# The first slice's first product taken by quarters of K between the heads of the first attention, on 512 columns

## The chip, the cores and the metric

The kernel runs on one core of a Trainium2 chip. Its time is the device time of one execution in microseconds (us), the median of several runs. TensorE multiplies (its weight loads run beside its matmuls and have rows of their own, PEld), VectorE (DVE), ScalarE (ACT) and GpSimd (POOL) do the elementwise work, and all DMAs are issued from SyncE (SP).

## What is computed

Three stages follow each other on 1152 tokens (2 batches of 576) and 512 features:

```python
scores = q @ k.T / 8                       # 2 batches, 8 heads, 576 positions, 64 wide
mask: heads 0-3: 0 <= rel < 32
      heads 4-7: 0 <= rel < 128 and rel % 4 == 0
x = softmax(scores) @ v                    # -> [1152, 512]
p = domain_probs / (domain_probs.sum(-1) + 1e-9)
x = sum over 4 experts e of p[:, e] * (relu(x @ w1[e]) @ w2[e])     # 512 -> 1024 -> 512
h = x @ w_in                               # 512 -> 2048; float64 weights
out = (h - tanh(h)) @ w_out
```

## The kernel before

**Precision and tiles.** Matmuls are in float32r. Each operand is split into a high part (a rounded copy) and a low part (the rest), and three matmuls, high x high, high x low and low x high, make one exact one. The tokens stand in two sets: 512 (g = 0) and 640 (g = 1). The two layers are cut into slices of 512 hidden features: 8 slices of the first layer pair, 4 of the second. In a slice the first product gives the hidden features, 4 tiles f of 128, and the second product (steps `y`) multiplies them with w2 into a sum per token block. The slices 0 and 1 (`EARLY`) are done for g = 0 alone first, with their first product taken whole (`whole`, L1177); later slices use a seven-product scheme (`product`, L1216) on differences of quarter blocks, whose operands t1 to t4 are prepared by `prep_upper` and `prep_lower` (L734, L742).

**The first attention.** The 8 heads of g = 0 stand in four pairs, two plain ones and two dilated ones. For a pair `scores` (L920) makes 32 small matmuls into two PSUM banks; `softmax` (L937) runs per head over DVE, ACT and POOL; `transposes` (L966) first issues 4 or 6 dummy matmuls on zeros (`keep_warm`, L903) and then 4 transposes, whose result ACT copies out; `values` (L995) multiplies with v, and ACT copies the result to `xf`. A pair gives one quarter of K (kk = 0 to 3) of x for the products. `first_attention` (L1422) writes the order out: scores of pairs 0 and 1, the transposes of head 0, the scores of pair 2, the transposes of heads 1 and 2, the scores of pair 3, the values of pair 0, and so on. Only after that does `prep_whole` (L755) split x into four operands of two halves of 256 tokens each: ACT copies the high part, DVE subtracts for the low part.

**The first product.** `whole(n, f, half)` takes one f and one half of the tokens: 4 quarters of K x 3 matmuls of 256 columns, 8 such groups per slice, and after the second half a relu that is split again (ACT and DVE). It needs all four quarters of x.

**Weights.** `w_load` (L1051) loads 512 KB at a time into a ring of four raw tiles; `w1_split` (L1079) copies the high part on ACT and subtracts on POOL.

**The order of the work.** All operations are recorded first and then ordered by a planner (`Order`, L353). TensorE's order is the program's; on the other engines `lay` (L414) picks, at each step, by an operation's due time (`late`), which `deadlines` (L378) counts back from TensorE's running sum. Costs are a model in `Engine.cost` (L319). The second attention (g = 1) and other work off TensorE's main line are put between the steps with `when(due, ...)` (L1398, L1465 to L1487): `due` is a time in the plan's own sum of step durations, counted from the first product's start, and the work goes ahead of the first step that begins at or after it.

```python
        if n < EARLY:
            return 1.44
        return 6 * (0.120, 0.146)[g]
...
    BEAT = 10.5
    for n in range(4):
        pair = Pair(kinds[1, n < 2], n % 2)
        due = 9.0 + BEAT * n
...
        when(due + 12.2, pair.last)
        for i in range(2):
            when(due + 13.8 + 1.6 * i, lambda pair=pair, i=i: pair.values(i))
```

Of the kernel before, what the change touches and what calls it, by code (L numbers as in the profile page):

```python
# [103 lines left out]
class Tile:  # L104


    def __init__(self, ring, shape, dtype, hosts=()):
# [4 lines left out]
        self.hosts = hosts  # L112
# [16 lines left out]
class View:  # L129
# [46 lines left out]

    def region(self):
# [25 lines left out]
class Op:  # L203
    __slots__ = (
        "n", "engine", "us", "emit", "before", "after", "tiles", "port", "late", "ready", "left",
        "start", "end", "landing", "tail", "data",
# [6 lines left out]
class Program:  # L213
# [3 lines left out]
    DMA_US, DMA_RATE, DMA_AHEAD = 2.0, 300.0e3, 0.36  # L217

    def __init__(self):
        self.ops = []  # L220
        self.open = None

    def op(self, engine, us, emit, outs=(), ins=(), port=False, data=0.0):
# [9 lines left out]
        o.before, o.after, o.tiles = set(), [], []  # L233
        o.tail = self.TAIL[engine]
# [61 lines left out]
class Engine:  # L296
# [22 lines left out]
    def cost(self, method, kw, outs, ins):  # L319
# [25 lines left out]
        if method == "tensor_tensor":  # L345
            return 0.185 + n * 0.00217, True
# [3 lines left out]
NAMES = ("tensor", "vector", "scalar", "gpsimd", "sync")  # L350


class Order:  # L353
# [6 lines left out]
    def __init__(self, program, rounds=3):  # L360
# [12 lines left out]
        self.follow = None  # L373
        for _ in range(rounds):
            self.deadlines()
            self.lay()

# [36 lines left out]
    def lay(self):  # L414

        ops = self.ops
        free = dict.fromkeys(NAMES, 0.0)
        port = path = 0.0
        lag = 0.0
        for ring in self.rings:  # L420
            ring.next = 0
            ring.free = [(0.0, i, None) for i in range(len(ring.slots))]
        for o in ops:
# [6 lines left out]
            o.start = o.end = None  # L430
        follow = {}
        waiting = {name: [o for o in ops if o.engine == name and not o.left] for name in NAMES}
        pe = [o for o in ops if o.engine == "tensor"]
        pe_next, done = 0, 0
        while done < len(ops):
            best = None
            for name in NAMES:
                if name == "tensor":
                    if pe_next == len(pe) or pe[pe_next].left:
                        continue  # L440
                    able = [pe[pe_next]]
# [3 lines left out]
                for o in able:  # L445
                    at = max(o.ready, free[name])
                    claims = {}
                    for t in o.tiles:
                        if t.slot_n is None:
# [3 lines left out]
                            if (  # L453
                                ring.next + k >= len(ring.tiles) or ring.tiles[ring.next + k] is not t
                                or k >= len(ring.free)
                            ):
# [8 lines left out]
                if not found:  # L465
                    continue
                first = min(f[0] for f in found)
                pick = min((f for f in found if f[0] <= first + 0.03), key=lambda f: f[1:3])
                if name != "tensor":
                    end = pick[0] + pick[3].us  # L470
                    for f in found:
                        if (
                            f[0] < end and f[1] < pick[1] - 0.5
                            and end > f[1] + lag - self.AHEAD
                            and pick[1] + lag > f[0] + f[3].us + pick[3].us * 0
                        ):
                            if best is None or True:
# [1128 lines left out]
```

## Time and profile before

| | |
|---|---|
| median of 3 runs | 632.15 us (631.94 to 632.74) |
| profiled execution | 632.89 us, span 631.1 us |
| TensorE busy | 620.2 us (98% of the span), 4093 matmuls |
| DVE, ACT, POOL busy | 406.6, 303.4, 332.7 us (64%, 48%, 53%) |
| DMA | 68.05 MB, mean 108 GB/s |
| mean granted TensorE clock | 0.996 |

The profiled execution's span runs from its first to its last instruction; the time of a run holds 1.8 us more around it. A busy share counts an engine's instructions, dummies among them, and matmul ends are modelled, so the pace of TensorE is read from starts of matmuls or of weight loads. Nearly all operations are emitted from one helper, line 312, so groups are told apart by tile names and shapes: `att` holds softmax tiles, `x` operands of x (and q and k before), `w` split weights, `h` hidden features (and v before), `acc` the plain x and later the sums, `raw` loaded weights.

### The profile page before, as it was taken

The page shows a single profiled execution, that of the slowest core. Times are in us where ns is not written, and L with a number is a line of the kernel's source. Part 1 is how long each engine was busy: PE and PEld are TensorE (multiplying, and loading weights), DVE is VectorE, ACT ScalarE, POOL GpSimd, SP SyncE. Part 2 cuts the span into 40 slices and gives each one's busy share as a digit, 9 for nine tenths or more (in the row PEclk, how much of TensorE's full clock was granted, in tenths as well). Part 3 has the DMA queues.
Part 4 walks back from the last instruction along what each step waited for, and adds up shares of the span by engine and source line. Part 5 has one row for each costly group of instructions (what it writes and reads, how often), then busy time and mean ns, then how long its engine had stood idle before and what let it go on. Part 6 is the DMA issues. An engine that isn't in the chain of part 4 may idle for free.

```text
span 631.1 us, 10738 instructions
## 1 busy us (share of the span) xinstructions
PE 620.2 (98%) x4093; PEld 545.6 (86%) x4093; DVE 406.6 (64%) x727; ACT 303.4 (48%) x720; POOL 332.7 (53%) x292
## 2 busy tenths in 40 slices
PE   7999999999999999999999999999999999999997
PEld 3598888989889889889889889898798988998985
DVE  5696647888987798725425458245998973653652
ACT  4758666456325325415315346353785661651540
POOL 5458876567524425524424448873476782570320
PEclk8999999999999999999999999999999999999999
DMA  8982216336465365112112112231507511200012
GB/s 322 346 268 58 78 38 198 102 119 215 134 186 175 113 201 166 62 51 66 35 34 68 33 34 68 83 114 73 166 11 215 160 50 51 68 1 1 18 51 83
DMA packets 36691, 68.05 MB, mean 108 GB/s; under 512 B 4128, under 2 KB 10400, under 8 KB 36640
## 3 DMA queue, kind: packets, MB, share of 16 engines
q1 hardware_dynamic: 36640, 67.37, 33.0%
q8 instruction: 32, 0.52, 0.3%
q14 instruction: 19, 0.16, 0.1%
HBM read 56.61 MB, written 10.75 MB: 107 GB/s over the span
## 4 chain that ended last, share of the span: by engine, by line
PE 85%; DVE 8%; POOL 2%; DMA 2%; ACT 1%; issue 1%; DVEq 0%; SPq 0%; POOLq 0%; ACTq 0%
PE bank L312 85%; DVE att L312 4%; DVE bank L312 1%; DVE x L312 1%; POOL h L312 1%; DMA att<-in_moe_w_out_dram 1%; DVE h L312 1%; DMA in<-att 1%; ACT att L312 1%; POOL att L312 0%; ACT h L312 0%; DVE w L312 0%; DVE st L312 0%; POOL w L312 0%; POOL sum L312 0%
## 5 line engine op out<-in xcount | busy, mean ns | idle before, releaser
L312 PE MATMUL bank<-w,h 128*128 128x512 f32 (+1 forms) x1392 | 322.1, 384 | 0.9 <-ACT h L312 0.7
L312 PE MATMUL bank<-x,w 128*128 128x256 f32 (+1 forms) x2040 | 288.3, 296 | 1.1 <-DVE bank L312 0.5
L312 PEld LDWEIGHTS bank<-x,w 128*128 128x128 f32 x2040 | 280.6, 189 | 9.7 <-DVE bank L312 0.9
L312 PEld LDWEIGHTS bank<-w,h 128*128 128x128 f32 (+1 forms) x1392 | 241.0, 185 | 51.6 <-POOL h L312 1.3
L312 POOL TENSOR_TENSOR w<-raw,w 128x512 fp32r<-128x512 f32 x102 | 139.0, 1379 | 138.1 <-ACT w L312 137.0
L312 ACT ACTIVATE h<-bank 128x320 fp32r<-128x320 f32 (+4 forms) x164 | 68.3, 427 | 88.3 <-PE bank L312 73.3
L312 DVE SCALAR_TENSOR_TENSOR acc<-bank,pn,acc 128x512 f32<-128x512 f32 x63 | 47.1, 749 | 76.4 <-PE bank L312 76.2
L312 DVE SCALAR_TENSOR_TENSOR att<-att 128x512 int32<-128x512 int32 (+1 forms) x96 | 89.5, 941 | 2.1
L312 ACT ACTIVATE w<-raw 128x512 fp32r<-128x512 f32 x112 | 69.0, 627 | 33.0 <-PE bank L312 30.6
L312 DVE TENSOR_TENSOR bank<-bank,p 128x320 f32<-128x320 f32 (+1 forms) x132 | 61.0, 466 | 32.2 <-PE bank L312 21.6
L312 DVE SCALAR_TENSOR_TENSOR h<-bank,h 128x320 fp32r<-128x320 f32 (+2 forms) x120 | 55.5, 474 | 21.8 <-ACT h L312 20.0
L312 POOL TENSOR_TENSOR w<-sum,w 128x512 fp32r<-128x512 f32 x36 | 47.7, 1324 | 37.1 <-ACT w L312 37.0
L312 ACT ACTIVATE p<-bank 128x320 f32<-128x320 f32 (+1 forms) x88 | 35.9, 412 | 55.4 <-PE bank L312 54.3
L312 ACT ACTIVATE att<-bank 128x256 f32<-128x256 f32 (+3 forms) x78 | 32.9, 433 | 50.1 <-PE bank L312 45.9
L312 POOL TENSOR_TENSOR h<-att,h 128x256 fp32r<-128x256 f32 (+1 forms) x32 | 30.4, 964 | 32.7 <-ACT h L312 32.0
L312 ACT ACTIVATE att<-att 128x512 f32<-128x512 f32 (+2 forms) x40 | 26.1, 652 | 35.4 <-DVE att L312 30.7
L312 DVE TENSOR_TENSOR acc<-bank,acc 128x512 f32<-128x512 f32 (+1 forms) x28 | 18.7, 672 | 36.3 <-PE bank L312 36.1
L312 POOL TENSOR_TENSOR att<-att,st 128x384 f32<-128x384 f32 (+1 forms) x24 | 21.7, 909 | 24.0 <-DVE st L312 21.8
L312 ACT ACTIVATE w<-sum 128x512 fp32r<-128x512 f32 x36 | 22.6, 626 | 16.4 <-PE bank L312 14.5
L312 POOL TENSOR_TENSOR sum<-raw 128x512 f32<-128x512 f32 x12 | 16.6, 1387 | 25.5 <-issue 8.7
L312 DVE TENSOR_SCALAR att<-att 128x512 int32<-128x512 int32 x32 | 19.0, 597 | 4.1 <-DMA in<-att 3.1
L312 DVE TENSOR_TENSOR bank<-bank,att 128x256 f32<-128x256 f32 (+1 forms) x32 | 14.5, 463 | 10.2 <-ACT att L312 9.8
(56 smaller groups left out, 361.6 us busy)
## 6 DMA issues: line engine op xcount, KB each, us to landing
raw<-in_moe_w_dram SPq DMA_DIRECT2D x40, 512.0 KB, 3.9
att<-in_moe_w_in_dram SPq DMA_DIRECT2D x16, 512.0 KB, 4.2
att<-in_moe_w_out_dram SPq DMA_DIRECT2D x16, 512.0 KB, 4.6
in<-att SPq DMA_DIRECT2D x16, 256.0 KB, 4.3
out<-att SPq DMA_DIRECT2D x16, 256.0 KB, 3.8
raw<-in SPq DMA_DIRECT2D x8, 512.0 KB, 3.8
raw<-out SPq DMA_DIRECT2D x8, 512.0 KB, 3.6
h<-in_v_dram SPq DMA_DIRECT2D x7, 512.0 KB, 7.3
```

Source lines behind the costliest of these rows:

```text
L312: getattr(self.engine, method)(**real)
```

## The change

The first product of slices 0 and 1 runs on 512 columns: x is kept as whole 512-column high and low tiles (`x_whole`), and `whole(n, f, kks)` takes any quarters of K. For slice 0 the quarters 0, 1 and 2 are recorded within the first attention (`some`) and marked as filling work; only quarter 3 follows as steps. Their four PSUM banks are claimed when wanted (`loose`) and stay open until quarter 3. For g = 0, `values` copies the high part from PSUM on ACT, subtracts the low part on DVE, and copies the plain x after that. All scores come ahead of the first transposes. `keep_warm` goes; `warm` records single dummy matmuls that the planner issues or leaves out. The high copies of slice 0's w1 go to DVE. Dilated q and k are loaded in halves, and v stands ahead of the first w1 load. The planner has start times per engine, other DMA constants, picks among the next 40 TensorE operations (filling work if it ends by the time the next fixed one can start), and tries 1200 random shifts of the due times of the operations up to the first product's last step, keeping those with the earliest end.

```diff
-    DMA_US, DMA_RATE, DMA_AHEAD = 2.0, 300.0e3, 0.36
+    DMA_US, DMA_RATE, DMA_AHEAD = 2.2, 360.0e3, 0.4
+
+    BEGIN = {"tensor": 0.9, "vector": 0.8, "scalar": 2.0, "gpsimd": 0.7, "sync": 0.75}
...
         for _ in range(rounds):
             self.deadlines()
             self.lay()
+        self.seek(program.seek, 1200)
+        self.lay()
...
+    def of_tensor(self, pe, found):
+
+        fixed = next((o for o in pe if not o.fill), None)
+        first = [f for f in found if f[3] is fixed]
+        idle = [f for f in found if f[3].fill == "idle"]
+        fill = [f for f in found if f[3].fill is True]
+        pick = first[0] if first else None
+        for some in (fill, idle):
+            if some:
+                f = min(some, key=lambda f: (f[0], f[2]))
+                if pick is None or f[0] + f[3].us <= pick[0] + self.OVER:
+                    pick = f
+        return pick
...
+    def x_whole(kk):
+
+        j = kk // 2
+        if ("whole", j) not in xop[0]:
+            t = [x_tile(0).rearrange("p a b q -> p a (b q)") for _ in range(2)]
+            xop[0]["whole", j] = t
...
-    def keep_warm(bank_, n):
-
+    def warm(n):
+
+        P.fill = "idle"
+        if 0 not in whole_:
+            whole_[0] = bank(True)
...
-                if self.h.g == 0 and (self.kk, a) != (3, 1):
-                    keep_warm(pb, 6 if self.kk == 3 else 4)
...
-            for dst, src in h.evict(i, xb, self.kk):
+            if h.g == 0:
+                hi, lo = x_whole(self.kk)
+                for dst, src in h.evict(i, xb, hi):
+                    copy(dst, src)
+                for (dst, src), (back, _) in zip(h.evict(i, xb, lo), h.evict(i, xb, hi)):
+                    sub(dve, dst, src, back.bitcast(F32))
+            for dst, src in h.evict(i, xb, xf[h.g][self.kk]):
                 copy(dst, src)
...
-        split(t[:, 0], t[:, 1], src, engine)
+        split(t[:, 0], t[:, 1], src, engine, None if n else dve)
...
-    def whole(n, f, half):
...
+    def whole(n, f, kks):
+
+        if f not in whole_:
+            whole_[f] = bank(n == 0)
+        b = whole_[f]
         with P.group():
...
+            for kk in kks:
+                w, x = w1t[n, f"a{f // 2 + 1}{kk // 2 + 1}"], x_whole(kk)
...
-        return [("h", n, g, i) for i in range(8 if n < EARLY else len(ORDER))]
+        return [("h", n, g, i) for i in range(NF if n < EARLY else len(ORDER))]
...
-            return 1.44
+            return 0.227 * (12 if n else 3)
...
-            whole(n, i // 2, i % 2)
+            whole(n, i, range(KD) if n else (3,))
...
+        def some(kk):
+            if not kk:
+                w1_all(0)
+                ready["w1"] = 0
+            P.fill = True
+            for f in range(NF):
+                whole(0, f, (kk,))
+            P.fill = False
+
+        warm(WARM)
         pairs[0].scores()
         soft(0, 1)
         pairs[1].scores()
-        soft(2)
+        soft(2, 3)
+        warm(12)
+        pairs[2].scores()
+        warm(12)
+        pairs[3].scores()
+        soft(4, 5)
+        warm(12)
         turn(0)
-        pairs[2].scores()
-        soft(3)
+        warm(12)
         turn(1)
-        soft(4)
+        warm(12)
         turn(2)
-        pairs[3].scores()
         pairs[0].values(0)
-        soft(5)
+        warm(12)
         turn(3)
-        soft(6)
+        soft(6, 7)
+        some(0)
         turn(4)
         pairs[1].values(0)
-        soft(7)
         turn(5)
         turn(6)
-        prep_whole(0, 0, False)
-        prep_whole(0, 1, False)
+        some(1)
         pairs[2].values(0)
-        prep_whole(0, 0, True)
         turn(7)
         pairs[3].values(0)
-        prep_whole(0, 1, True)
-
+        some(2)
...
-    da.load_q()
-    for u in range(2):
-        da.load_k_cut(u)
+    for c in range(2):
+        da.load_q(slice(c, c + 1))
+        da.load_k_cut(c)
+    for i in range(2):
+        pa.load_v(i)
     w_load(0, 0)
     for i in range(2):
-        pa.load_v(i)
+        da.load_v(i)
     w_load(0, 1)
```

## Rows read from the trace of the kernel before

**Rows 1.** The page: the span in 40 slices, busy tenths.

```profile
PE   7999999999999999999999999999999999999997
...
DMA  8982216336465365112112112231507511200012
```

**Rows 2.** Stretches of 5 us: PE, PEld, DVE, ACT, POOL busy (instructions), clock, DMA share, GB/s.

```profile
10.00:15.00 5.00, 4.37 (x44) 2.52 (x44) 3.80 (x12) 2.43 (x10) 3.13 (x5) 0.66 1.03 404
15.00:20.00 5.00, 5.00 (x82) 3.10 (x80) 2.13 (x6) 2.92 (x11) 2.40 (x3) 1.00 1.02 386
20.00:25.00 5.00, 4.63 (x52) 2.57 (x51) 3.56 (x10) 4.21 (x14) 2.15 (x3) 1.00 1.09 328
25.00:30.00 5.00, 4.22 (x66) 2.87 (x66) 4.56 (x8) 4.43 (x9) 3.60 (x4) 1.00 0.97 333
```

**Rows 3.** The chain that ended last, first 45 us: start, us, what.

```profile
10.63 9.57 PE bank L312 x124
...
32.43 12.71 PE bank L312 x132
```

**Rows 4.** Timeline of TensorE, 5 to 46 us: start, us, operation, idle before.

```profile
10.63 0.64 PE L312 MATMUL bank<-ident,att 128*96 128x128 f32 x4 [2.36 <-POOL att L312]
11.20 1.43 PE L312 MATMUL bank<-x,x 64*64 64x96 f32 x32
12.56 1.89 PE L312 MATMUL bank<-zero 128*32 128x512 bf16 x4
...
16.68 0.89 PE L312 MATMUL bank<-x,x 64*64 64x96 f32 x32
...
20.12 1.04 PE L312 MATMUL bank<-zero 128*32 128x512 bf16 x4
...
21.66 1.15 PE L312 MATMUL bank<-w,h 96*64 96x64 f32 x32
...
30.52 0.97 PE L312 MATMUL bank<-x,w 128*128 128x256 f32 x6
...
41.76 1.05 PE L312 MATMUL bank<-x,x 64*64 64x96 f32 x40
...
44.27 2.03 PE L312 MATMUL bank<-w,h 128*128 128x512 f32 x8
```

**Rows 5.** One stretch of 256-column matmuls: its length and its weight loads (PEld).

```profile
62.26:66.53 4.27, 4.27 (x36) 1.00 0.28 95
```

**Rows 6.** Timeline around the last first-attention copy and the last second-attention values.

```profile
30.63 1.08 ACT L312 ACTIVATE acc<-bank 128x512 f32<-128x512 f32 x1 [0.63 <-PE bank L312]
...
105.15 9.60 PEld L312 LDWEIGHTS bank<-w,h 128*128 128x128 f32 x42
...
113.22 0.48 DVE L312 TENSOR_TENSOR x<-acc,x 128x320 fp32r<-128x320 f32 x1
...
114.80 7.32 PEld L312 LDWEIGHTS bank<-x,w 128*128 128x128 f32 x49
```

**Rows 7.** Groups of DVE, 0 to 36 us: busy us, mean ns, idle before.

```profile
L312 DVE TENSOR_TENSOR x<-acc,x 128x256 fp32r<-128x256 f32 x8 | 3.0, 419 | 1.9 <-ACT x L312 1.8
...
L312 DVE CAST p<-p 128x384 bf16<-128x384 f32 x1 | 0.4, 360 | 1.6 <-POOL p L312 1.6
```

**Rows 8.** Instructions on the weight tiles, 30 to 60 us: ns min/median/max.

```profile
L312 POOL TENSOR_TENSOR w<-raw,w x8: 1279/1290/1759, 33.7 to 58.5; 128x512 fp32r<-128x512 f32 x8
L312 DVE TENSOR_TENSOR w<-raw,w x2: 1239/1422/1606, 37.0 to 41.1; 128x512 fp32r<-128x512 f32 x2
```

**Rows 9.** Timeline of SP: the first issues of weight loads.

```profile
7.00 2.70 SPq L605 DMA_DIRECT2D raw<-in_moe_w_dram  x3
```

**Rows 10.** DMA issues from 7.0 to 8.2 us: KB each, median us to landing.

```profile
raw<-in_moe_w_dram SPq DMA_DIRECT2D x2, 512.0 KB, 10.8
```

**Rows 11.** Timeline of POOL, 40 to 60 us: start, us, operation, idle before.

```profile
47.91 1.01 POOL L312 TENSOR_TENSOR att<-att,st 128x480 f32<-128x480 f32 x1 [4.95 <-DVE st L312]
...
54.77 5.02 POOL L312 TENSOR_TENSOR w<-raw,w 128x512 fp32r<-128x512 f32 x4
```

More of the change, by code (lines that the diff above doesn't have):

```diff
@@ L175, in real, with real_strides @@
         return ap
+    def real_strides(self):
+        at = self.at
+        return [
+            1 if n == 1 else int(np.take(at, 1, axis=i).flat[0] - np.take(at, 0, axis=i).flat[0])
+            for i, n in enumerate(at.shape)
+        ]
     def region(self):
@@ L205 @@
         "n", "engine", "us", "emit", "before", "after", "tiles", "port", "late", "ready", "left",
-        "start", "end", "landing", "tail", "data",
+        "start", "end", "landing", "tail", "data", "fill", "gone",
     )
@@ L345, in cost @@
         if method == "tensor_tensor":
-            return 0.185 + n * 0.00217, True
+            spread = any(0 in v.real_strides() for v in ins)
+            return 0.185 + n * (0.00168 if spread else 0.00217), True
         return 0.1 + n * 0.0025, True
 NAMES = ("tensor", "vector", "scalar", "gpsimd", "sync")
+class Stuck(Exception):
+    pass
 class Order:
@@ L420, in lay @@
         for ring in self.rings:
+            ring.left = [t for t in ring.tiles if not t.loose]
             ring.next = 0
@@ L452, in lay @@
                             claims[ring] += 1
[L453 to L456, printed above, removed]
+                            if k >= len(ring.free) or not (t.loose or (
+                                ring.next + k < len(ring.left) and ring.left[ring.next + k] is t
+                            )):
                                 at = None
@@ L501, in lay @@
                     ring = t.ring
[L502 removed]
+                    ring.next += not t.loose
                     ring.free.sort()
@@ L519, in lay, with leave, stuck @@
             done += 1
-        self.follow = follow
-        self.us = max(o.end for o in ops)
-    def stuck(self, waiting, pe, pe_next):
-        said = [f"pe {pe_next}/{len(pe)} left {pe[pe_next].left if pe_next < len(pe) else None}"]
-        if pe_next < len(pe):
-            said.append(str([(t.ring.name, t.slot_n) for t in pe[pe_next].tiles]))
-            said.append(str([ops.n for ops in (self.ops[b] for b in pe[pe_next].before) if ops.start is None]))
+        if limit is None:
+            self.follow = follow
+        self.us = max(o.end for o in ops if o.engine == "tensor")
+    def leave(self, o, at):
+        o.start = o.end = o.landing = at
+        o.gone = True
+        for t in o.tiles:
+            t.left -= 1
+        for n in o.after:
+            a = self.ops[n]
+            a.left -= 1
+            assert a.engine == "tensor"
+    LOOK = 40
+    OVER = 0.1
+    def of_tensor(self, pe, found):
[8 more added lines that the diff above has]
+                if pick is None or f[0] + f[3].us <= pick[0] + self.OVER:
+                    pick = f
+        return pick
+    def stuck(self, waiting, pe):
+        said = [f"pe {len(pe)} left {pe[0].left if pe else None}"]
+        if pe:
+            said.append(str([(t.ring.name, t.slot_n) for t in pe[0].tiles]))
         for name, found in waiting.items():
@@ L619, in copy, with split @@
         act.activation(out=out, in_=in_, func=ACTF.Copy)
-    def split(hi, lo, src, engine):
-        copy(hi, src)
+    def split(hi, lo, src, engine, first=None):
+        if first is dve:
+            dve.tensor_copy(out=hi, in_=src)
+        else:
+            copy(hi, src)
         sub(engine, lo, src, hi.bitcast(F32))
@@ L981, in transposes @@
             to = self.pt.setdefault(a, t[:, 1])
-            copy(to[:BK], pb[:BK])
+            if False:
+                dve.tensor_copy(out=to[:BK], in_=pb[:BK])
+            else:
+                copy(to[:BK], pb[:BK])
         def last(self):
@@ L1517, in tile_local_attention_moe_tanhshrink @@
     db.load_v_short()
-    idle = bank()
-    with P.group():
-        keep_warm(idle, WARM)
     first_exp = const("first_exp", [128, 32], BF16)
```

148 lines of the change are left out of this document (90 added, 58 removed).

## The prediction, made before the change was run

> **What bounds the kernel now.** I read first the slices of the page [rows 1], to see where TensorE is not full: in the first slices only. The digit is 9 from the third slice to the last but one, and DMA is busy in the first three. Whatever shortens the time must therefore either cut TensorE's work after the head, or move it into the head. The cut by 5 us shows what the head is made of [rows 2]: TensorE shows 4.2 to 5.0 us busy of 5, but at 10 to 15 us at a granted clock of 0.66, and DMA is at its limit (share about 1, 330 to 400 GB/s). The chain of waits [rows 3] then says that the head is not one engine's: softmax steps alternate with a piece of 9.57 us on TensorE, and from 32.43 us on TensorE alone carries the end. The timeline of TensorE [rows 4] shows what those pieces hold: transposes (0.64), scores (0.89; 1.43 in the slow stretch), values (1.15), and between them groups of dummy matmuls on zeros, four taking 1.04 and in the slow stretch 1.89. These dummies are the gap: time in which TensorE is counted busy and does nothing. The first slice's first product begins at 30.52 and ends where the second product begins, at 44.27. Of that, some 1.0 is the scores of the second attention at 41.76, so I call its end E = 43.3, the scores left out.
>
> **The change, part by part.**
>
> *512 columns instead of 2 x 256.* 36 matmuls of 256 columns go from 62.26 to 66.53, 0.1186 each [rows 5]; 42 of 512 columns from 105.15 to 114.80, 0.230 each [rows 6]. The first product of an early slice was 96 x 0.1186 = 11.4 and becomes 48 x 0.230 = 11.0. In the second slice, where nothing else of it changes, that is a gain of 0.3 to 0.4; I take 0.3.
>
> *Three quarters of K moved into the head.* The first slice's product falls into four quarters of 12 x 0.230 = 2.76. Quarters 0, 1 and 2 are filling work: 36 matmuls, 8.3 us, put wherever the next attention step isn't ready. Only the last quarter must follow the last attention output. Two things bound the new E.
>
> From the chain's side: the last values end at about 30.6 and ScalarE copies them out in 1.08 (strided, from 30.63) [rows 6]. After the change that first copy is already the high part, and one VectorE step of 128x512 from PSUM makes the low part; no row shows that step, so it lies between two of the 128x256 steps (2 x 0.42 [rows 7]) and the longest 128x512 step, 1.61 [rows 8]. I take 0.9, nearer to the two halves since they compute the same. So without any shortening of the attention x is ready at 30.63 + 1.08 + 0.9 = 32.6 (high end 33.3), and E = 32.6 + 2.76 = 35.4. How much does the attention itself shorten? The fixed dummies between the transposes leave the order, and all scores come ahead. In the 9.57 us piece of the chain lie three dummy groups (the 1.89 one, and two as the one of 1.04), 3.9 us. All of that gone is one bound, nothing the other; I take 1.6, under the half, because VectorE (4.56 of 5 busy at 25 to 30) and ScalarE (4.43) would be late next [rows 2]. E = 33.8 by this side, 31.5 to 36.1 by its ends.
>
> From TensorE's side: quarter 0 can't start before the first w1 block is in and split. Before, the first loads of w1 are issued at 7.00 [rows 9] and take 10.8 to land [rows 10], so 17.8, plus one copy and one GpSimd step (1.29, with 1.76 at most [rows 8]): 19.7. The change puts the first values' loads ahead of it and the others' behind, so about 1 MB less lies before it (128 x 2048 floats of dilated values), which at the 400 GB/s of [rows 2] is 2.6: about 17. At 17 four transposes and two and a half values are left by my count, 4 x 0.57 (the step from 10.63 to 11.20) + 2.5 x 1.15 = 5.2, and 11.0 of product: 17 + 16.2 = 33.2 if TensorE never idles. From 19.7 with one more pair done it is 34.7. Both sides meet at 33 to 35; I take E = 33.8, a gain of 9.5, with 11.8 and 7.2 as ends.
>
> *The split of w1 and of x.* The four high copies of w1 go from ScalarE to VectorE. No row shows such a copy: between 0.36 (a 128x384 cast) and 1.61 (the longest 128x512 step) [rows 7, 8], so 1.4 to 6.4 for four; I take 2, by the cast, which has one input as they have. Against it stand eight x steps of 0.42 that become four of 0.9: about even. VectorE has to place those 2 us between 10 and 30 us, where it is busy 3.80 + 2.13 + 3.56 + 4.56 of 20 [rows 2]: the 6 us idle are the cover, and if that is gone, the chain's side above gets later by them, which the bound of 36.1 holds. ScalarE copies each output twice, as high part and as plain x; the second copy isn't awaited by the product.
>
> *More, smaller loads.* The dilated q and k come in halves: four more issues on SP, some 0.9 each by the three weight loads of 2.70 [rows 9], ahead of values and weights. The queue's engines are full anyway, so they cost nothing while they stay full; otherwise up to 3.6 on quarter 0, again inside the bound.
>
> *What follows sooner.* The second product of slice 0 starts some 9.5 us earlier, but the second attention's steps are placed by plan time from the start of the first product, so they don't move earlier by as much. Its last values stood 9.65 us before the first product on the second token set: from 105.15 to 114.80 lies most of a second product [rows 6]. In the change the first slice's eight plan steps of 1.44 become four of 0.68, so every later step has a plan time some 9 smaller, and the last values come directly ahead of that first product: the cover is gone. There, 24 matmuls of 320 columns at 7.32 / 49 = 0.15 [rows 6] (3.6 us) remain until the first operand that needs these values. I charge 1.0 for it; the bounds are under rival 1.
>
> *The clock.* TensorE is idle for 2.36 us before 10.63, and the next scores take 1.43 against 0.89 [rows 4]; the stretch has 0.66 granted [rows 2], a mean of the two levels, 1.2 and 2.4 GHz. The change drops the fixed dummies ahead of each transpose and puts dummies only where the planner models a gap. One such dip costs about 1.5 (0.54 of scores, 0.85 of dummies, some of transposes), and I leave the one that is there.
>
> **Sum.** -9.5 - 0.3 + 1.0 = -8.8. The profiled execution took 632.89 (span 631.1 and 1.8 around it), so 624.1; the median of the runs is 0.74 lower, so 623.4. About 0.2%, 1.3 us, is what a measurement of this kernel can tell from no change.
>
> **Rivals.**
>
> 1. *The second attention becomes the wait.* For it: from the last values' end at 105.15 to the end of the last step that prepares the second x at 113.70 (113.22 + 0.48) pass 8.55 [rows 6]; if the awaited operand were the last of them, TensorE would wait 8.55 - 3.6 = 4.9. Against it: the steps ran late there because nothing asked for them. The stall is 0 to 4.9; at about 4 the time is some 626.5, and with E at its late end 629.
>
> 2. *GpSimd holds the second slice.* Its four w1 splits run from 54.77 to 59.79, two are needed for the first group, and that group started about when two were done (54.77 + 2 x 1.25 = 57.3) [rows 11]. If that can't move, TensorE gains at the first product and waits it out there: only 0.3 and some tenths remain, 631.5. Against it: GpSimd idled 4.95 us before 47.91, and the splits had no haste.
>
> 3. *The quarters don't fit.* If the first w1 block lands or is split so late that the quarters run after the last x, the change doesn't do what it says: E = 31.0 + 11.0 = 42.0, and the time is 632.15 - 1.3 - 0.3 = 630.5. For it speak the landing time of 10.8 and the full DMA; against it that 1 MB can go behind.
>
> 4. *The clock falls, slower.* Between 10.6 and E lie 8.9 us of attention and 11.0 of product. If the planned gaps differ from the real ones, TensorE idles as before 10.63 and runs the work at 1.2 GHz. Each microsecond of work so run costs one more, some 3.3 of them in idle time; the change turns to a loss from about 13 us of the 20 on. With 15: 12 more, 635. For it speaks that the only dip of the head came right after an idle stretch, though a dummy group preceded it [rows 4]; against it that from 15 us on the clock held at 1.00 [rows 2], and that the quarters make the head denser. The Trainium skill (TensorE: Matmul & The Clock Gate, "The HAM clock gate") says the throttled state is the default and activity releases it, which speaks against taking dummies out; the dip after idling agrees [rows 2, 4]. By that rule, were the real work too thin, the time would be this rival's.
>
> **How the numbers follow.** Forecast (both sides of E at 33 to 35, small stall): 0.60, own range 619.8 to 626.5. Rival 1: 0.19. Rival 2: 0.06. Rival 3: 0.06. Rival 4: 0.09. Faster is the forecast with rivals 1 and 3, 0.85; no change is rival 2, 0.06; slower is rival 4, 0.09. The range goes from E at 31.5 with no stall (632.15 - 11.8 - 0.3, about 619.8) to E at 36.1 with a stall of 4.4 (632.15 - 7.2 - 0.3 + 4.4 = 629.0); rivals 2 to 4 stay out of it.
>
> **What would show it.** Right: 48 matmuls of 512 columns of the first slice's x and w, 36 of them ahead of the last values; no more than 12 of them after; the second product starting at 34 to 35 instead of 44.27; about the same TensorE pace thereafter, so that every later stage lies 9 us earlier. Rival 1 shows as idle TensorE a few groups into the first product on the second token set, released by VectorE or ScalarE; rival 2 as idle before the second slice's first group, released by GpSimd; rival 3 as a solid 11 us of product after the last values; rival 4 as a granted clock well under 1 from 15 to 35 us. The prediction is wrong if the second product starts after 37, or if the 9 us gained there are not found at the end.

## The result and the profile after

The change made the kernel slower: 638.30 us, median of 4 runs (637.73 to 638.71), beside 632.05 (631.61 to 632.74) for the kernel before; the ratio is 1.0097, with a 95% interval of 1.008 to 1.0115. The profiled execution took 638.29, span 636.5, mean granted clock 0.984 (before: 632.89, 631.1 and 0.996). The forecast was 623.4. Two executions of this document, 675.79 (kernel before) and 755.69 (e10_gate_warm_low_first), ran at a granted clock of 0.85 and 0.754 and are left out of every median.

The slices of the page after, to be laid beside [rows 1] (PEclk is the granted clock in tenths):

```profile
PE   8769999999999999999999999999999999999997
...
PEclk9769999999999999999999999999999999999999
```

The loss is in the head again: the second and third slices of TensorE are lower than they were, and everything behind them is full as before. The stretches of 5 us of the kernel after (columns as in [rows 2]) show when there is a dip, a stretch at the lower clock:

```profile
15.00:20.00 5.00, 2.82 (x43) 1.89 (x41) 4.00 (x10) 3.33 (x12) 3.22 (x4) 0.93 1.03 340
20.00:25.00 5.00, 3.56 (x38) 2.97 (x39) 4.07 (x13) 2.42 (x10) 3.35 (x5) 0.50 1.01 365
25.00:30.00 5.00, 5.00 (x23) 4.07 (x22) 4.27 (x7) 4.37 (x11) 3.04 (x3) 0.88 0.72 223
30.00:35.00 5.00, 3.94 (x48) 2.87 (x46) 2.19 (x6) 2.81 (x4) 1.25 (x2) 1.00 0.74 189
35.00:40.00 5.00, 1.96 (x22) 1.46 (x24) 4.93 (x6) 0.90 (x2) 5.00 (x6) 0.64 0.97 377
40.00:45.00 5.00, 3.82 (x24) 2.65 (x21) 2.37 (x5) 2.00 (x2) 1.28 (x2) 0.50 1.04 401
45.00:50.00 5.00, 5.00 (x13) 3.84 (x13) 1.48 (x3) 2.10 (x4) 0.00 (x0) 0.50 0.59 220
```

From 15 to 25 us TensorE had 5.00 and 4.63 busy of 5 at a clock of 1.00 [rows 2]; now it has 2.82, then 3.56 at a granted 0.50, which is the lower level, 1.2 GHz, throughout. From 35 to 40 us it has 1.96, and the 10 us behind that run at 0.50 again. The timeline of TensorE after, to be laid beside [rows 4], names the places:

```profile
21.44 1.08 PE L324 MATMUL bank<-ident,att 128*96 128x128 f32 x4 [3.61 <-POOL att L324]
22.45 1.98 PE L324 MATMUL bank<-w,h 96*64 96x64 f32 x32
24.36 3.17 PE L324 MATMUL bank<-x,w 128*128 128x512 f32 x9
...
27.72 3.00 PE L324 MATMUL bank<-x,w 128*128 128x512 f32 x12
...
32.17 0.96 PE L324 MATMUL bank<-x,w 128*128 128x512 f32 x3
32.97 0.60 PE L324 MATMUL bank<-ident,att 128*96 128x128 f32 x4
33.44 0.50 PE L324 MATMUL bank<-x,w 128*128 128x512 f32 x1
35.44 0.73 PE L324 MATMUL bank<-x,w 128*128 128x512 f32 x2 [1.50 <-DVE x L324]
36.09 0.33 PE L324 MATMUL bank<-att,h 96*64 96x64 f32 x2
39.03 1.97 PE L324 MATMUL bank<-att,h 96*64 96x64 f32 x30 [2.60 <-ACT att L324]
40.92 2.08 PE L324 MATMUL bank<-x,w 128*128 128x512 f32 x4
44.18 6.89 PE L324 MATMUL bank<-x,w 128*128 128x512 f32 x17 [1.18 <-DVE x L324]
50.91 8.52 PE L324 MATMUL bank<-w,h 128*128 128x512 f32 x36
```

The quarters are there: 9 + 12 + 3 + 1 + 2 + 4 + 17 = 48 matmuls of 512 columns. But TensorE stands still for 3.61 us ahead of head 4's transposes, and the values that follow take 1.98 where they took 1.15 in [rows 4]. It stands still for 2.60 within the last values, between the first 2 of their 32 matmuls and the other 30, which then take 1.97. The last 17 matmuls of the product take 6.73 from start to start, 0.40 each, where 0.23 was the pace [rows 6]. The second product starts at 50.91, where it started at 44.27, or 43.3 without the scores ahead of it: E is 7.6 later.

Why the last values wait so long is seen on ScalarE, in its timeline after:

```profile
25.80 2.19 ACT L324 ACTIVATE w<-raw 128x512 fp32r<-128x512 f32 x4
...
28.84 0.52 ACT L324 ACTIVATE att<-att 128x384 f32<-128x384 f32 x1
...
33.15 1.13 ACT L324 ACTIVATE acc<-bank 128x512 f32<-128x512 f32 x1
34.06 0.44 ACT L324 ACTIVATE x<-acc 128x256 fp32r<-128x256 f32 x1
38.08 0.42 ACT L324 ACTIVATE x<-acc 128x256 fp32r<-128x256 f32 x1 [3.58 <-DVE acc L324]
38.40 0.57 ACT L324 ACTIVATE att<-bank 96x512 f32<-96x512 f32 x1
41.03 1.08 ACT L324 ACTIVATE x<-bank 128x512 fp32r<-128x512 f32 x1 [2.06 <-PE bank L324]
41.90 1.12 ACT L324 ACTIVATE acc<-bank 128x512 f32<-128x512 f32 x1
```

Head 7's transposes are done at 33.57 (32.97 + 0.60); the copy that takes them out, at 38.40, comes 4.8 us later. ScalarE idled in between, with the wrong instruction at the head of its queue: a copy of 256 columns into an operand that the third slice will use (`x<-acc`), planned ahead of head 7's copy, which waits for a step on VectorE (`acc<-acc`) that prepares it. The timeline of VectorE after:

```profile
34.32 1.06 DVE L324 TENSOR_TENSOR x<-bank,x 128x512 fp32r<-128x512 f32 x1 [2.74 <-DMA x<-in_k_dram]
35.41 1.19 DVE L324 CAST p<-p 64x96 bf16<-64x96 f32 x1
36.62 1.42 DVE L324 TENSOR_TENSOR acc<-acc 128x256 f32<-128x256 f32 x1
...
43.06 1.06 DVE L324 TENSOR_TENSOR x<-bank,x 128x512 fp32r<-128x512 f32 x1 [2.06 <-ACT acc L324]
```

VectorE reaches that step (36.62) after the low part of the third quarter and a mask cast for the second attention. The low part is needed for the first product; the cast, the step at 36.62 and ScalarE's copies of `x<-acc` are not. So the wait that bounds the head now runs from later work on VectorE, through later work on ScalarE, to the last head.

The stages behind the first product lost nothing. From 55 us on TensorE waits 0.9 us in all (0.7 and 0.2, both behind 449 us), and from E to the end of the span it takes 636.5 - 50.9 = 585.6, where it was 631.1 - 43.3 = 587.8: 2.2 less. Of these, 0.5 are two waits for VectorE that only the kernel before has; the rest was not taken apart.

### The profile page after: what moved, and what is told of

Read it like the earlier page. It is cut to its first block, busy times and chain, and to the rows that moved or that the text cites. A ratio compares the mean times of both kernels' runs of the same rounds, so it can differ in the third digit from the quotient of the medians.

```text
span 636.5 us, 10517 instructions
## 1 busy us (share of the span) xinstructions
PE 621.0 (98%) x3985; PEld 542.9 (85%) x3985; DVE 410.5 (64%) x727; ACT 302.1 (47%) x712; POOL 330.9 (52%) x292
## 4 chain that ended last, share of the span: by engine, by line
PE 92%; DMA 3%; SPq 2%; DVE 1%; issue 0%; ACT 0%; POOL 0%; DVEq 0%
PE bank L324 92%; DMA x<-in_k_dram 2%; SPq L692 2%; DMA raw<-in_moe_w_dram 1%; DVE acc L324 0%; DVE x L324 0%; POOL h L324 0%; DVE w L324 0%; DVE p L324 0%; ACT acc L324 0%; ACT att L324 0%; DVE bank L324 0%; DVE att L324 0%; ACT h L324 0%; DVEq L1718 0%
## 5 line engine op out<-in xcount | busy, mean ns | idle before, releaser
L324 PE MATMUL bank<-x,w 128*128 128x320 f32 (+2 forms) x1944 | 292.0, 304 | 2.7 <-DVE x L324 2.7
L324 PEld LDWEIGHTS bank<-x,w 128*128 128x128 f32 x1944 | 277.5, 190 | 16.1 <-DVE x L324 3.5
L324 ACT ACTIVATE w<-raw 128x512 fp32r<-128x512 f32 x108 | 66.9, 628 | 41.1 <-PE bank L324 39.1
L324 DVE SCALAR_TENSOR_TENSOR att<-att 128x512 int32<-128x512 int32 (+1 forms) x96 | 84.5, 899 | 2.2 <-ACT att L324 0.7
L324 POOL TENSOR_TENSOR att<-att,st 128x384 f32<-128x384 f32 (+1 forms) x24 | 21.9, 913 | 17.1 <-DVE st L324 11.3
L324 DVE TENSOR_SCALAR att<-att 128x512 int32<-128x512 int32 x32 | 24.7, 776 | 5.5 <-DMA out<-att 5.1
```

What stands on the lines that cost most here:

```text
L324: getattr(self.engine, method)(**real)
```

## The experiments

Each kernel changes the kernel after, and each computes the same output; they add dummy matmuls or change where work stands. Ratios are to the kernel before, run on the same chip in the same session (median 632.29 to 632.55). The last three columns are starts on TensorE: of the last pair's values (the 30 matmuls, where 2 ran ahead), of the last piece of the first product, and of the second product. They are those of one profiled execution each, and in that they differ by chance: with the same order up to there, head 4's transposes start at 21.44 in the kernel after, at 20.67 in e6_last_copy_first and at 22.27 in e7_low_part_first. A difference of about 1 us in one position therefore shows little.

| | us (runs) | ratio, 95% | last values | last quarter | second product |
|---|---|---|---|---|---|
| after | 638.30 (4) | 1.0097 [1.0080, 1.0115] | 39.03 | 44.18 | 50.91 |
| e1_gate | 629.92 (10) | 0.9969 [0.9953, 0.9985] | 30.70 | 35.02 | 39.10, stops for 1.09 |
| e2_warm | 632.33 (10) | 1.0010 [0.9992, 1.0028] | 36.12 | 40.47 | 43.81 |
| e3_late_quarters | 635.28 (5) | 1.0069 [1.0043, 1.0094] | 30.86 | | 45.8 without scores |
| e4_gate_warm | 630.23 (10) | 0.9984 [0.9968, 0.9999] | 29.68 | 34.45 | 39.21 |
| e5_dummies_same_order | 636.35 (4) | 1.0051 [1.0012, 1.0090] | 36.96 | 42.12 | 47.75 |
| e6_last_copy_first | 634.01 (8) | 1.0029 [1.0013, 1.0045] | 34.78 | 39.81 | 43.86 |
| e7_low_part_first | 635.93 (7) | 1.0053 [1.0036, 1.0070] | 39.05 | 43.31 | 49.36 |
| e8_all_three | 629.89 (8) | 0.9961 [0.9946, 0.9976] | 34.03 | 37.46 | 41.53 |
| e9_gate_late | 636.68 (4) | 1.0072 [1.0044, 1.0100] | 29.11 | | 44.4 without scores |
| e10_gate_warm_low_first | 631.75 (9) | 0.9990 [0.9977, 1.0003] | 29.87 | 35.19 | 39.95 |
| e11_other_seed | 638.47 (4) | 1.0094 [1.0076, 1.0111] | 37.38 | 41.73 | 44.39, stops for 5.0 |
| e12_gate_scalar_copies | 637.32 (4) | 1.0072 [1.0051, 1.0092] | 36.27 | 40.66 | 44.02, stops for 3.9 |

**Later work kept behind the attention.** On VectorE, ScalarE and GpSimd the planner may not pick anything recorded after the first attention until the engine's own share of it is done (the gate, below).

```diff
+                    if core[name]:
+                        able = [o for o in able if o.n < self.program.core]
...
     first_attention()
+    P.core = len(P.ops)
```

> Edit: on VectorE, ScalarE and GpSimd the planner may issue later work (operand preparation, w2 splits, mask casts) only after the last instruction of the first attention on that engine. Theory Q (queues: the late copy of the last head at 38.40 stood behind later work in ScalarE's queue): the last values start near 34 instead of 39.0, the second dip of the clock (35 to 49 us) goes or shrinks, the first slice's second product starts at about 43 instead of 50.9, the time is about 631. Theory C (clock: the idle 3.6 us before 21.44 and the dip of 20 to 26 us are the root): the dip stays as it was, the second product starts at 47 or later, the time is 635 to 637. Theory P (VectorE and GpSimd contend in the head, from the w1 split): as C, without a change of the dip's place.

The timeline of TensorE in e1_gate:

```profile
30.70 1.15 PE L324 MATMUL bank<-att,h 96*64 96x64 f32 x30 [0.29 <-ACT att L324]
...
35.02 4.24 PE L324 MATMUL bank<-x,w 128*128 128x512 f32 x17 [1.34 <-DVE x L324]
39.10 1.08 PE L324 MATMUL bank<-w,h 128*128 128x512 f32 x4
41.27 7.69 PE L324 MATMUL bank<-w,h 128*128 128x512 f32 x32 [1.09 <-DVE w L324]
```

The last values stand 8.3 us earlier, the granted clock is 1.00 in every stretch of 5 us from 10 to 50 us, and the second product begins 11.8 earlier, though it then stops for 1.09 on a weight split that the gate put off. VectorE had less to do in the head, 17.41 us of the 28 from 6 to 34 us, where the kernel after has 21.00. This one rule makes the kernel faster than before (by 0.3%) and after. The gate was not tried on the kernel before, so what it would give without this change is not known.

**Dummies in the gap.** The same planner, with 16 dummies that it may place ahead of the first quarter:

```diff
+        warm(16)
         some(0)
```

> Edit: 16 optional dummy matmuls recorded between the transposes of head 3 and the first quarter, for the gap before 21.44. Theory C: the granted clock stays 1.00 from 20 to 25 us, the values of the second pair take 1.15 instead of 1.98 and a group of three 512-column matmuls 0.7 instead of 1.1 to 1.3; every later attention step comes some 3 us sooner, the second product starts at 45 to 48, the time is 632 to 635. Theory Q: the clock is held but the last head's copy still stands behind later work, so the last values still start at 36 or later and the time stays above 634. Theory P: the clock is held and nothing else moves, 637 to 638.

The clock is 1.00 in every stretch from 10 to 50 us, and the second product starts at 43.81, 7.1 earlier. The last values still start at 36.12, as theory Q has it, but the time is not above 634. The planner's whole order changed with the edit, so these 7.1 are not the clock's price alone. That was tried in the exact order of the kernel after, with 14 dummies put ahead of head 4's transposes (operation 241; 62 is a dummy) as the instructions are emitted:

```diff
+            if o.n == 241:
+                for _ in range(14):
+                    self.ops[62].emit()
```

> Edit: the order of the changed kernel is kept on every engine; 14 dummy matmuls are issued ahead of head 4's transposes, where TensorE idled 3.6 us. Theory C, clean: the granted clock stays 1.00 to 33 us, the second pair's values take 1.15 instead of 1.98 and quarter 0's groups 0.7 each, so head 5's transposes come at 25.5 instead of 27.4 and the later ones move with it only as far as the other engines let them; the second dip after 35 us stays, because the wait of 36.4 to 39 stays. Second product at 47 to 49, time 634 to 636. If the clock of the first dip is all, 44 and 632. If the clock costs nothing, 50.9 and 638.

TensorE's timeline in e5_dummies_same_order:

```profile
36.96 1.97 PE L324 MATMUL bank<-att,h 96*64 96x64 f32 x30 [2.59 <-ACT att L324]
```

The first dip is gone (clock 1.00 up to 35 us), and all of the head moves 2 to 3 us: last values -2.1, second product -3.2. The 2.59 us wait for head 7's copy is still there, and so is the second dip behind it (0.54 and 0.50 from 35 to 45 us). The price of the first dip is thus about 3 us at E. In time it is less sure: the median is 1.95 lower, but the four runs go from 634.04 to 637.79 (the profiled one) and the interval overlaps that of the kernel after.

**The order on ScalarE alone.** In the exact order of the kernel after, the two `x<-acc` copies (operations 296 and 316) and the steps on VectorE and GpSimd that belong to them (315 and 297) are put behind head 7's copy:

```diff
+        moved = {296: 32.70, 315: 32.71, 316: 32.72, 297: 32.73}
+        for n, at in moved.items():
+            self.ops[n].start = at
```

> Edit: the order is kept but for one place: ScalarE's two copies that prepare the third slice, and the two subtractions they need, go behind the last head's and the last pair's copies instead of ahead of them. Theory Q, clean: the last head's copy moves from 38.40 to about 34.4, the last values from 39.0 to about 36.1, the second product from 50.9 to 47 or, if the shorter idle also keeps the clock at 1.00, to 43. Time 634 or 630.5. If the copy was late for another reason (VectorE's or a load's), it stays above 37 and the time at 637 to 638.

ScalarE's timeline in e6_last_copy_first has head 7's copy directly behind its neighbour:

```profile
31.82 1.14 ACT L324 ACTIVATE acc<-bank 128x512 f32<-128x512 f32 x1
32.74 0.64 ACT L324 ACTIVATE att<-bank 96x512 f32<-96x512 f32 x1
```

The last values stand 4.3 earlier and the second product 7.0; of these 1.3 were there ahead of the edit's place (head 7's transposes began at 31.63 instead of 32.97). The rest at the second product is more than the 2.60 of the wait, because the product behind it runs at the full clock again (17 matmuls in 4.05 instead of 6.73), from 39.81 to 43.86 on TensorE:

```profile
39.81 4.22 PE L324 MATMUL bank<-x,w 128*128 128x512 f32 x17 [1.23 <-DVE x L324]
```

The profiled execution, 631.48, was the fastest of eight that reach 635.89, and its mean granted clock, 0.994, the highest (the others 0.987 to 0.991), so the median's gain, 4.3, is the better measure.

**The low part ahead of the plain copy.** In the kernel after, the last quarter's low part on VectorE starts at 43.06, when ScalarE's plain copy of the same bank ends, and not when the high copy that it needs does (41.03 + 1.08). The order of the two was turned for the last two quarters (264 and 258 are their plain copies):

```diff
+        moved = {264: 32.80, 258: 28.42}
```

> Edit: the order is kept but for the last two pairs' plain copies of x, which ScalarE now issues behind VectorE's low part instead of ahead. The low parts began at 34.32 and 43.06, 0.04 after the end of that copy and 0.9 after the end of the high part. If the two readers of one bank go one after the other, in the order they are issued, the low part of the last pair starts 0.03 after the high part and all that follows comes 0.9 to 1.8 earlier: second product at 49 to 50, time 636.5 to 637.5. If VectorE waited for something else, no change.

VectorE's timeline in e7_low_part_first:

```profile
42.19 1.07 DVE L324 TENSOR_TENSOR x<-bank,x 128x512 fp32r<-128x512 f32 x1 [1.18 <-ACT x L324]
```

and ScalarE's in the same kernel:

```profile
41.06 1.09 ACT L324 ACTIVATE x<-bank 128x512 fp32r<-128x512 f32 x1 [2.06 <-PE bank L324]
43.29 1.09 ACT L324 ACTIVATE acc<-bank 128x512 f32<-128x512 f32 x1 [1.13 <-DVE x L324]
```

The low part starts 0.04 after the high copy's end and the plain copy now waits for it: the two readers of one bank go one after the other, in program order. The rows show it as a wait of the one for the other; whether both could read at once was not tried. The second product is 1.55 earlier, though the last values are not: 0.9 is the last quarter's earlier low part (from the values to the last quarter 4.26 instead of 5.15), and 0.7 is the clock (the 17 matmuls take 6.05 instead of 6.73). This also corrects a releaser in the kernel after: the 2.74 put down to a DMA ahead of 34.32 ends with the plain copy (33.15 + 1.13).

**All three together.** e5, e6 and e7 in one kernel, the rest of the order untouched:

> Edit: all three. If the three are separate and add up, the second product starts at 40 to 42 and the time is 628 to 630; if the clock is what the other two act through, it is no earlier than the best one alone less 1 us.

The second product stands at 41.53, 9.4 earlier, where the three alone sum to 3.2 + 7.0 + 1.55 = 11.8. The granted clock is 1.00 from 10 to 50 us, so what e5, e6 and e7 each gain at the second dip can come in only once; that this is all of the difference was not shown. That is 1.8 ahead of before, and the time is as good as with the gate.

**Gate and dummies.**

> Edit: both of the first two, later work held behind the attention and 16 optional dummies in the first gap. If Q and C together are the cause, the clock stays near 1.00 through the head, the second product starts at 37 to 40 and the time is 624 to 628. If each covers the other (one root), it is no better than the better one of the two. Theory P: above 633.

No further gain: where the gate has taken the lateness out, the clock holds without the dummies (0.999 in both).

**What the quarters in the head are worth.** The calls that record them there are taken out, so that the whole first product follows the attention; once with the planner of the change, once with the gate.

```diff
-            P.fill = True
-            for f in range(NF):
-                whole(0, f, (kk,))
-            P.fill = False
```

> Edit: only the 512 columns, the attention's new order and its conversions are kept; the quarters 0 to 2 of the first slice are not taken in the head, the whole first product follows the last values. If the quarters are what slows the head (they stand ahead of transposes on TensorE at half the clock), the last values come sooner than 39.0, near 33, and the second product starts near 45 to 47, time about 633. If the head is slow by its other engines and the new order, the last values stay at 38 or later, the second product starts at 53 to 55 and the time is 641 to 643.

> Edit: later work held behind the attention as in the first run, and the quarters 0 to 2 not taken in the head. Measures what the moved quarters are worth on their own, with the queues clean. If they are work laid into time that was free, the last values start within 0.5 of the 30.7 of the first run, and the second product starts 36 matmuls less the 7 or 8 left over there, some 6 us, later: at 46, time 635 to 636. If the quarters delay the attention (TensorE or the early split of w1), the last values start at 28 to 29.5, the second product at 43 to 45 and the time is 632 to 634.

TensorE's timeline in e9_gate_late:

```profile
29.11 1.97 PE L324 MATMUL bank<-att,h 96*64 96x64 f32 x30 [0.34 <-ACT att L324]
31.01 13.46 PE L324 MATMUL bank<-x,w 128*128 128x512 f32 x48
```

With the gate the first product ends at 44.4 without the quarters in the head and at 40.2 with them (39.10 and the stop of 1.09): 4.2 us, for 8.3 us of work moved, and part of the 4.2 is the clock, which was at 0.50 to 0.69 from 20 to 35 us in e9_gate_late. The last values start 1.6 sooner without the quarters (29.11; 30.70 with them), although at the lower clock: the quarters do delay the attention, as the second branch of the expectation had it. That kernel's total is worse than both branches because TensorE waits 3.02 for VectorE at 152 us and runs 60 matmuls in 10.95 behind that, at a clock of 0.66 (8.20 in the kernel before). Without the gate, the quarters put the last values from 30.86 (e3_late_quarters) to 39.03 and E from 45.8 to 50.9: there they made it worse. Later work costs time in e3_late_quarters too: TensorE waits 3.78 ahead of 27.12 for ScalarE, whose four weight copies (23.93, 2.18) stand ahead of two heads' copies. How much of the loss goes to the quarters and how much to later work is not known, since the planner's order changed with the edit.

**Turning the low part under the gate.**

> Edit: the fourth run (later work held, 16 dummies) and the low parts of the last two pairs ahead of their plain copies, order else kept. If the readers of a bank go one after the other, the last quarter starts 0.9 earlier than 34.45 and the second product at 38.3 instead of 39.2; the time 629.0 to 629.7, the best so far. If ScalarE's plain copy is wanted sooner elsewhere, no gain: 630 to 630.5.

ScalarE's timeline in e10_gate_warm_low_first:

```profile
32.94 1.10 ACT L324 ACTIVATE x<-bank 128x512 fp32r<-128x512 f32 x1
```

No gain: the third quarter's plain copy now waits 1.14 for its low part and runs from 32.07, and the last quarter's high copy stands behind it (31.29 in e4_gate_warm). Moving a wait helps only if nothing awaited is queued behind it.

**Is it one unlucky order?** The planner searches with random shifts; another seed gives another order.

```diff
-        chance = random.Random(1)
+        chance = random.Random(2)
```

> Edit: only the seed of the planner's random search, 1 to 2; what is computed and recorded is the same. If the result of the change is a draw (a plan near its optimum whose tight places meet real durations by chance), the second product starts anywhere between 42 and 51 and the time lies between 630 and 638 and differs from 638.3 by over 2. If the loss is in the change whatever the plan, it starts at 49 to 52 and the time is 637 to 639.

The same time by another place of the same kind; two seeds are all that was tried. ScalarE's timeline in e11_other_seed:

```profile
44.49 0.63 ACT L324 ACTIVATE w<-raw 128x512 fp32r<-128x512 f32 x1 [0.70 <-DMA raw<-in_moe_w_dram]
45.84 1.67 ACT L324 ACTIVATE w<-raw 128x512 fp32r<-128x512 f32 x3 [0.72 <-DMA raw<-in_moe_w_dram]
47.42 1.93 ACT L324 ACTIVATE x<-acc 128x256 fp32r<-128x256 f32 x6
49.26 1.05 ACT L324 ACTIVATE h<-bank 128x512 fp32r<-128x512 f32 x2
```

The copy that the second product needs (`h`) stands behind four weight copies that wait for their loads and six operand copies; TensorE, started at 44.39, stops for 3.94 and for 1.03.

**The w1 copies back on ScalarE.** The gate, and slice 0's high copies of w1 on ScalarE as they were:

```diff
-        split(t[:, 0], t[:, 1], src, engine, None if n else dve)
+        split(t[:, 0], t[:, 1], src, engine)
```

> Edit: later work held as in the first run, and the high copies of the first slice's w1 back on ScalarE (0.62 each there, 0.56 to 0.75 on VectorE). If VectorE's copies, in contention with GpSimd, set the pace of the head, the last values start at 29 to 30 and the second product at 38 to 39, time 628.5 to 629.5. If ScalarE sets it (18.3 of 28 us busy in the head against VectorE's 17.4), the last values start 1 to 2 later, the second product at 41 to 43, time 631 to 633.

TensorE's timeline in e12_gate_scalar_copies:

```profile
48.56 5.92 PE L324 MATMUL bank<-w,h 128*128 128x512 f32 x13 [3.92 <-DVE h L324]
```

7.4 us slower than the gate alone, each taken against the kernel before in its session: TensorE waits 2.88 for head 4's softmax step at 20.66, the clock falls (0.57 from 20 to 25 us), and the second product, started at 44.02, waits 3.92. In these two orders VectorE is the better place for the copies; the planner made a new order for each, so the copies' own price is not shown.

## Why the prediction was wrong, step by step

The sum was -8.8 and the median moved +6.25. The failing step is E: forecast 33.8, measured 50.9, with a high end of 36.1. Its three pieces, by their starts on TensorE: the last values were to end at 29.0 and ended at 40.9 (11.9 late); from there to the last quarter 2.0 was forecast (the high copy and the low part) and 3.3 went by (1.2 late); the last quarter was to take 2.76 and what was left took 6.73 (4.0 late). That is all of the 17.1. Behind E the sum added 0.7 (-0.3 and 1.0) and the profiled execution took 2.2 less, so 17.1 - 2.9 is its miss of 14.2. (The low end of the range is 620.05 by its own sum, not 619.8.)

- *"I take 1.6" for the shortening of the attention.* This failed most. I asked whether the attention's own steps would get shorter and took 0 as the pessimistic end. I had no case in which they get later, because I read the order of the other engines as given. Their order comes from the planner too, and it puts work of later slices between the attention's steps on ScalarE and VectorE. When it ran, that work stood at the head of the queue and head 7's copy behind it. e6_last_copy_first shows it by moving four later steps behind that copy, and e1_gate by keeping all such work behind. Head 4's transposes were hardly later than in the kernel before (21.44; 21.09 then), but head 7's 5.2 later (32.97; 27.77 then). TensorE's timeline of the kernel before:

```profile
21.09 0.64 PE L312 MATMUL bank<-ident,att 128*96 128x128 f32 x4
...
27.77 0.64 PE L312 MATMUL bank<-ident,att 128*96 128x128 f32 x4
```

  With the first dip gone they were at 31.82 (e5_dummies_same_order), with the gate, which keeps the clock too, at 28.12 (e1_gate): most of the lateness is the queues', not the clock's. The queue can be seen there as well: ScalarE's last softmax step of head 7 runs at 28.84 in the kernel after, behind four weight copies (25.80, 2.19), and at 24.93 in e1_gate, where no such copy runs before 33.67. Even with the queues clean (e4_gate_warm) the last values end at 31.2: no shortening at all, 2.2 behind the forecast.
- *"I leave the one that is there" for the clock.* It had two dips in place of one, the first behind 3.61 us of idle TensorE, the second behind 1.50 and 2.60. Rival 4 described this, and its 635 was the nearest of all the times; I gave it 0.09. That nearness is in part luck: the first dip is worth about 3 us at E (e5_dummies_same_order), and the second came from the queues, which the rival did not have. Its argument against, that the quarters make the head denser, failed because the first quarter came at 24.36, behind the gap and not in it, where 17 to 19.7 was forecast. Its operands weren't there earlier: the low part of x was done at 21.45 on VectorE (20.77 and 0.68), the weight splits on GpSimd at 20.18 and 23.92 (18.90 and 1.28, 22.65 and 1.27). The Trainium skill (TensorE: Matmul & The Clock Gate, "HAM oscillation — how this bites in real kernels") says that waits between groups of matmuls throttle the clock again, and the work after them starts cold; the trace agrees, with 0.50 granted from 20 to 25 us behind the 3.61.
- *"The second copy isn't awaited by the product".* It is, by way of VectorE: the low part starts after it, 0.9 us later than it could for the last quarter (e7_low_part_first).
- *The low part, 0.9.* 1.06 where x is written in strides, as for the dilated pairs; 0.68 plain. The groups of VectorE after, from 6 to 36 us:

```profile
L324 DVE CAST w<-raw 128x512 fp32r<-128x512 f32 x4 | 2.7, 691 | 0.0
...
L324 DVE TENSOR_TENSOR x<-bank,x 128x512 fp32r<-128x512 f32 x3 | 2.4, 812 | 4.1 <-DMA x<-in_k_dram 2.7 <-ACT x L324 1.4
```

- *w1's copies, 2 us.* 2.7, within the bounds of 1.4 to 6.4; with them on ScalarE the kernel was slower (e12_gate_scalar_copies). This step held.
- *"Only the last quarter must follow."* At most 12 were to run behind the last values. 21 of the 48 did, 17 of them from 44.18 on; in e4_gate_warm it was 30, and the last 20 took 4.76 instead of 2.76. In that kernel the three pieces are 2.2, 1.3 and 2.0 late, and E is 39.2. So of the forecast gain of 9.5 at E the change holds 3 to 4 with the gate (40.2 in e1_gate, 39.2 in e4_gate_warm, 43.3 before), and the rest of the miss, 11.7, goes with queue order and clock.
- *512 columns, and the later stages.* 17 matmuls in 4.05 at the full clock (e6_last_copy_first), 0.238 each where 0.230 was forecast. 48 of them are 11.4, as long as the 96 x 0.1186 of before: the 0.3 for the second slice is not borne out by this pace. The stall of 1.0 did not come, nor did rivals 1 and 2: TensorE waits for nothing between 55 and 449 us. But the head had nothing to hand on there. Where E is 3 to 4 earlier than before, in e1_gate and e4_gate_warm, TensorE waits only 0.2 from 45 to 190 us, which speaks against rivals 1 and 2; a wait for VectorE appears only at 192 us (0.44 and 0.92), and of 1.7 in e8_all_three and e5_dummies_same_order, at 194 and 200 us. Rival 3 did not occur: 31 of 48 matmuls ran before the last wait.

What stays open is how the planner's order and its expected times drift apart: which step is first late by how much was not taken apart, only where it ends. The planner's own new parts (the start times, the DMA constants, the random shifts) were not tried one by one, nor on the kernel before. That an executed order other than these could reach the forecast's 33.8 was not tried.

## What to carry to other kernels

Before you fill gaps of an engine that works in order, ask what the filling stands in front of when the times slip: keep work of later stages off the queues of the engines that feed the critical chain until that chain is done; one such rule turned 638.3 into 629.9, below the 632.3 of before. Work moved into a gap of TensorE fills it only if its operands are there when the gap is; until they are, dummies kept the clock here (1.00 with 14 of them, 0.50 without). And when a step "moves nothing but an order", read who shares a bank or a queue with it.

## What the hardware showed that I had not expected

A small step on VectorE can wait for GpSimd. In the kernel after, a sum of 128x4 elements beside a weight split on GpSimd, in the timelines of both:

```profile
19.08 1.11 DVE L324 TENSOR_TENSOR st<-st,eps 128x4 f32<-128x4 f32 x1
```

```profile
18.90 1.28 POOL L324 TENSOR_TENSOR w<-raw,w 128x512 fp32r<-128x512 f32 x1 [1.33 <-DVE w L324]
```

Both end at about 20.19; the same sum took 0.16 at 22.49. It lies on the softmax of head 4, ahead of the 3.61 us gap. The step at 36.62 that ScalarE waited for (a sum of 128x256) took 1.42 beside GpSimd's three splits from 35.27 to 39.16, and 0.40 at 26.49. The Trainium skill (SBUF — State Buffer, "SBUF: two separate sides") says that GpSimd and a VectorE operation with two inputs in SBUF lock a shared pair of ports for a whole instruction; the trace agrees, by the common end of the two rows above. VectorE's timeline in e9_gate_late, where neither a split nor a weight copy stands at this place:

```profile
18.30 0.15 DVE L324 TENSOR_TENSOR st<-st,eps 128x4 f32<-128x4 f32 x1
```

Head 4's transposes start at 19.69 there, 1.75 earlier than in the kernel after, and TensorE waits 1.97 for them instead of 3.61. By the rows about 1.0 of this is the longer sum, and most of the rest two casts on VectorE ahead of it (18.41 and 18.85, 0.42 and 0.20 long), the first a w1 copy that the change put there. What this is worth in the kernel's time was not measured by itself.
